# A gated feed-forward beside linear attention: the last 64 input rows of the first feed-forward product join its Strassen products

## The chip, the cores and the metric

The kernel runs on one core of a Trainium2 chip. A core has a matrix engine (TensorE, in the profile PE, its weight loads PEld), three engines for elementwise work (VectorE or DVE, ScalarE or ACT, GpSimd or POOL) and SyncE (SP), which here issues every data transfer (DMA). Each engine runs its own instructions in order and waits for the others on semaphores. Operands lie in an on-chip memory of 128 partitions; TensorE writes its results into banks of a second memory, PSUM, 512 fp32 values a partition each. The metric is the device time of one execution in microseconds.

## The reference

The input is x, 2048 tokens of 576 values. Cut to what matters:

```python
xn = layernorm(x)                       # [2048, 576]
q, k, v = split(xn @ wqkv)              # 32 heads of 18
s = linear_attention(phi(q), phi(k), v) @ wo
h = gelu(xn @ w1 + b1)                  # w1: [576, 4608], the first feed-forward product
g = silu(h @ w2 + b2)                   # w2: [4608, 576]
out = x + s * g
```

The change touches `xn @ w1` (its inner dimension is 576 = 512 + 64) and the place where `b2` is added.

## The kernel before

**Precision.** All matrix products are made from fp32 values split in two reduced-precision halves: `hi` is the value cast down (ScalarE), `lo` is what the cast lost (a VectorE difference of the value and `hi`). A product is hi x hi + hi x lo + lo x hi, three matmuls for every block of 128 inner rows.

**Stages.** First loop over 16 tiles of 128 tokens: layernorm, transposes, k, v, the state of the attention; meanwhile operands of w2 are prepared and stored. Second loop, `for i in range(1, NT + 4)`: queries, denominators, the attention output; beside it (function `beside(i, k)`, tables `SUMS` and `SPLITS`) the sums of token blocks that the feed-forward part needs. Then the feed-forward part: 18 steps. The tokens are handled in two halves of 1024; half 0 of the loop (steps 0 to 8) works on tokens 1024 to 2047, whose operands are on chip, and the other 1024 tokens' operands lie in DRAM (`x_dram`) and are loaded at the end of step 8 (`load_x_part`). A step makes 512 of the 4608 columns of h: two "up" products (class `Up`, 256 columns of w1 each), then a "down" product with the matching rows of w2 (function `product`), summed in `macc`.

**Strassen products.** Up and down products use a Winograd form of Strassen's scheme: seven products of sums of blocks in place of eight products of blocks. In an up product the two blocks of columns are `f0`, `f1`, the two blocks of 512 tokens are 0 and 1, and the inner dimension is split in A (rows 0 to 255) and B (rows 256 to 511). The weight sums 5, 6, 7, 4 are differences made by GpSimd (method `T`: T5 = f1A - f0A, T6 = f1B - T5, T7 = f1B - f1A, T4 = f0B - T6); "a" holds f0 itself (products 1 and 2), "b" the B part of f1 (product 3). The seven products are issued in the order `UP = (1, 6, 7, 5, 2, 3, 4)`. Product 1 goes into bank A and is copied by ScalarE to `m1_sb`; product 2 is added in the same bank. Product 6 and m1 give u1, product 7 and u1 give u2 (VectorE). Product 5 goes into bank E; VectorE adds it and u2 into B; then product 3 is accumulated on bank E.

**The last 64 rows.** 576 = 512 + 64, and the 64 rest rows are outside the scheme: with hi and lo stacked in one tile of 128 partitions, each of the four results gets two more matmuls (`rest` in `mm`: products 5, 2, 3 and 4). The difference of the two token blocks that product 3's bank needs is made by `XSums.rest`.

**Weights.** In steps 0 to 8 each 256 columns of w1 are prepared once (class `W1`: raw load, `T`, `hi`, `lo`) and stored to DRAM; steps 9 to 17 load the ready operands (`W1Loaded`). The plan of a step has 28 slots: slots 0 to 6 and 7 to 13 follow the products of its two up products, slots 14 to 27 the fourteen pieces of the down product. `P1` says in which slots the second operand of this step is prepared (during the first up product), `P0` where the first operand of the next step is. What is planned in a slot is issued after the product of that slot and what reads it. `in_order` fixes the order of VectorE, ScalarE, GpSimd and TensorE as issued; the transfers on SP are ordered by a scheduler. The lines to follow in the profile: L817 up matmuls, L834 copy of m1, L843 addition into B, L616 hi casts, L619 lo differences, L641, L643, L646, L649 T5, T6, T7, T4, L948 down matmuls, L955 their addition to `macc`, L337 and L341 token sums and their splits.

**The down product** has its own seven products in the order `ORDER = (1, 2, 7, 4, 5, 3, 6)`; 2, 4 and 3 are accumulated on the banks of 1, 7 and 5 after VectorE has read those. Each is made in two pieces of 256 tokens, each one bank pair out of three. In the first chunk of a half `macc` is begun: by a copy, or with the bias b2 (`BIAS`, a broadcast tile `b2b`).

Of the kernel before, what the change touches and what calls it, by code (L numbers as in the profile page):

```python
# [24 lines left out]
KT = 5  # L25
NF = F // P
# [13 lines left out]
def linear_attention_gated_ffn(ctx, tc, x, wqkv, wo, w1, b1, w2, b2, out):  # L40
# [4 lines left out]
    w1r = ctx.enter_context(tc.tile_pool(name="w1r", bufs=2))  # L45
# [32 lines left out]
    def stage_w1(name):  # L78
        return w1r.tile([P, 2 * KT * P], F32, tag="stw", name=name)

# [13 lines left out]
    b2b = pers.tile([P, D], F32, name="b2b")  # L94
# [19 lines left out]
    x_dram = dram.tile([P, 31, 512], F32, name="x_dram")  # L114
# [13 lines left out]
    wkvp = ph1.enter_context(tc.tile_pool(name="wkvp", bufs=1, reuse_waits="tile"))  # L128
    w2p = ph1.enter_context(tc.tile_pool(name="w2p", bufs=2, reuse_waits="tile"))
# [30 lines left out]
    def load_x(t):  # L160
        xraw[t] = stage_w1(f"x{t}")[:, :D] if t < 2 else stage(D, f"x{t}")
        nc.sync.dma_start(xraw[t], x[t * P : (t + 1) * P, :])
# [127 lines left out]
    def w2_hi(j):  # L290
        shape = [P, 2, 2, HD]
        if j % 4 < 2:
            w2op[j] = w1r.tile(shape, F32R, tag="stw", name=f"w2o{j}")
        else:
            w2op[j] = w2p.tile(shape, F32R, tag="w2o", name=f"w2o{j}")
        nc.scalar.copy(w2op[j][:, 0], w2_block(j // 3, T_OPS[j % 3])[0])
# [17 lines left out]
    class XSums:  # L314
# [8 lines left out]
        def place(self, in_place):  # L323
            A, B = self.A, self.B
            if in_place:
# [3 lines left out]
                self.xd = self.h0[:, 4]  # L329
            else:  # L330
                s2, s1, s4 = self.tiles = x_hi(0, "s2"), x_lo(0, "s1"), x_lo(1, "s4")
                self.s1, self.s2, self.s4 = ((t[:, A], t[:, B]) for t in (s1, s2, s4))
                self.xd = s2[:, 4]
# [30 lines left out]

        def rest(self, k):
            if k == 0:
                self.v = v, w = stage(512, "xv"), stage(512, "xw")
                self.tt(v, self.h0[:, 4], self.h1[:, 4], SUB)
                nc.sync.dma_start(w[:64], v[64:])
                nc.sync.dma_start(w[64:], v[:64])  # L370
                return
            (v, w), xd = self.v, self.xd
            if k == 1:
                self.tt(v, v, w, ADD)
            else:
                nc.scalar.copy(xd, v)
                self.tt(xd[64:], v[64:], xd[64:], SUB)

    def tmp_w1(name):
        return as2(stage_w1(name)[:, :1024])  # L380
# [29 lines left out]
    for t in range(NT):  # L410
# [43 lines left out]
        if t in (4, 8):  # L454
            b = t // 4 - 1
            if b == 0:
                nc.sync.dma_start(x_dram[:, 0:5], xh[0].bitcast(F32))
                nc.sync.dma_start(x_dram[:, 5:9], xl[0].bitcast(F32))
            else:
                nc.sync.dma_start(x_dram[:, 11:14], xh[1][:, 2:].bitcast(F32))  # L460
                nc.sync.dma_start(x_dram[:, 16:18], xl[1][:, 2:].bitcast(F32))
    xsum[0] = XSums(0, tmp_w1)
    xsum[0].sum1(0)
    nc.sync.dma_start(b1c, b1)
    nc.sync.dma_start(b2b, bass.AP(tensor=b2.tensor, offset=b2.offset, ap=[[0, P], [1, D]]))
# [12 lines left out]

    w1p = ctx.enter_context(tc.tile_pool(name="w1p", bufs=2, reuse_waits="tile"))
    w2rp = ctx.enter_context(tc.tile_pool(name="w2rp", bufs=1, reuse_waits="tile"))  # L480

    def load_w2_raw(n):
        raw = w2rp.tile([P, CF // 2, 2, 2, HD], F32, tag="w2raw", name=f"w2raw{n}")
        nc.sync.dma_start(raw.rearrange("p a b n d -> p (a b n d)"), w2[n % NC])
        return raw

# [57 lines left out]
    def normalize(t):  # L544
# [16 lines left out]
        if t:  # L561
            beside(t, 1)
# [47 lines left out]
    def keep_op(table, key, t, shape):  # L610
        d = dram.tile([P, 2, *shape], F32, name="op_" + "_".join(str(k) for k in key))
# [8 lines left out]

    class W1:


        def __init__(self, n):
# [3 lines left out]
            r4 = raw.rearrange("p (n k c) -> p n k c", n=2, k=KT)  # L628
            self.f0, self.f1 = r4[:, 0], r4[:, 1]
            self.src = {"a": self.f0, "b": self.f1[:, 2:]}  # L630
            self.ops, self.tiles = {}, {}

        def T(self, i):

            a, b = slice(0, 2), slice(2, 4)
            f0, f1, src = self.f0, self.f1, self.src
            tt = EW1.tensor_tensor
            if i in (5, 6):
                src[i] = w1p.tile([P, 2, P], F32, tag=f"w1t{i}", name=f"w1t{i}", bufs=1)
            if i == 5:  # L640
                tt(src[5], f1[:, a], f0[:, a], op=SUB)  # L641
            elif i == 6:
# [652 lines left out]
```

## Time and profile before

| | us |
|---|---|
| three runs | 1112.8, 1112.86, 1113.61 (median 1112.86) |
| the profiled execution | 1112.83 |
| its span, first to last instruction | 1111.0 |
| 0 to about 150 | first loop |
| about 150 to 290 | second loop |
| about 290 to 674 + 22 | steps 0 to 8 |
| about 696 to 1080 | steps 9 to 17 |
| after 1080 | the last down product and the output |

The granted TensorE clock was 0.999 of full speed. A row of a timeline gives start, length, engine, line, operation, output and inputs with their shapes, and in brackets how long the engine had been idle and what ended that. A row of waits gives who waited for whom, the total, how often and the longest. Instructions of one engine that follow closely overlap in the records by some hundredths of a microsecond, and matmuls by more, since they are pipelined; so the distance between starts is the price of a matmul.

### The profile page before, as it was taken

To read this page: it belongs to the slowest core of one execution; us is meant where nothing else is said; L and a number is where in the kernel's file an instruction comes from. 1 tells how busy PE (TensorE), PEld (TensorE's weight loads), DVE (VectorE), ACT (ScalarE), POOL (GpSimd) and SP (SyncE) were. 2 spreads that over 40 slices of the span, in tenths; PEclk is the share of its full clock that TensorE was granted. 3 is DMA by queue.
4 is the path that set the end of the run, shared out by engine and by line. 5 is a ranking of instruction groups with operands and counts; after the bars stand their busy time and mean duration, and the time that the engine had idled before them with its cause. 6 is when DMAs were issued, how large, how long until landed. Compare 5 with 4: busy or idle time off the path is not lost.

```text
span 1111.0 us, 18615 instructions
## 1 busy us (share of the span) xinstructions
PE 1101.8 (99%) x7008; PEld 1024.7 (92%) x7008; DVE 811.3 (73%) x1184; ACT 456.4 (41%) x800; POOL 448.8 (40%) x366
## 2 busy tenths in 40 slices
PE   8999999999999999999999999999999999999998
PEld 8999999999898998989989899899898998989987
DVE  6666657888697887988879878666475574764866
ACT  4444444233554354454544545524233242242342
POOL 4556534233354552553535524324234143242340
PEclk9999999999999999999999999999999999999999
DMA  7588631152757649476485679977666666666252
GB/s 298 190 334 301 237 123 44 71 215 93 283 227 282 239 176 356 162 264 243 182 333 184 231 283 397 353 251 263 227 207 211 206 203 213 228 201 222 83 164 101
DMA packets 83223, 246.71 MB, mean 222 GB/s; under 512 B 9213, under 2 KB 19709, under 8 KB 79551
## 3 DMA queue, kind: packets, MB, share of 16 engines
q1 hardware_dynamic: 83135, 245.54, 61.8%
q8 instruction: 55, 0.90, 0.3%
q14 instruction: 33, 0.27, 0.1%
HBM read 151.62 MB, written 92.47 MB: 220 GB/s over the span
## 4 chain that ended last, share of the span: by engine, by line
PE 95%; DVE 3%; POOL 1%; ACT 0%; DMA 0%; issue 0%; SPq 0%; POOLq 0%; DVEq 0%; ACTq 0%
PE pm L948 34%; PE e L817 12%; PE a L817 10%; PE zy L817 10%; PE pv L219 5%; PE pk L219 5%; PE b L817 4%; PE pq L219 4%; PE ps_s L592 4%; PE pd L1068 2%; PE ps_kva L256 1%; PE pt L196 1%; PE ps_kw L518 1%; PE ptp L574 1%; DVE xt L337 0%; DMA w<-wqkv 0%
## 5 line engine op out<-in xcount | busy, mean ns | idle before, releaser
L955 DVE TENSOR_TENSOR macc<-pm,macc 128x576 f32<-128x576 f32 x218 | 164.3, 754 | 56.8 <-PE pm L948 56.2
L616 ACT CAST h_h<-g 128x512 fp32r<-128x512 f32 x204 | 120.8, 621 | 139.9 <-PE pm L948 138.8
L619 DVE TENSOR_TENSOR h_l<-g,h_h 128x512 fp32r<-128x512 f32 x204 | 161.4, 798 | 0.0
L916 POOL TENSOR_TENSOR mid<-g 128x512 f32<-128x512 f32 x34 | 44.1, 1296 | 164.2 <-ACT g L825 164.2
L825 ACT ACTIVATE g<-b,b1c 128x512 f32<-128x512 f32 x36 | 24.8, 688 | 112.8 <-DVE b L843 112.7
L910 POOL TENSOR_TENSOR g<-g 128x512 f32<-128x512 f32 x34 | 55.0, 1618 | 34.1 <-DVE h_l L619 32.8
L834 ACT COPY mid<-a 128x512 f32<-128x512 f32 x36 | 21.1, 586 | 109.3 <-PE a L817 109.3
L837 DVE TENSOR_TENSOR mid<-b,mid 128x512 f32<-128x512 f32 x36 | 24.8, 690 | 46.5 <-PE b L817 35.4
L817 PE MATMUL a<-h0r,wa 128*128 128x512 f32 x180 | 58.6, 390 | 0.0
L817 PE MATMUL a<-xh,wa 128*128 128x512 f32 x180 | 58.5, 390 | 0.0
L913 POOL TENSOR_TENSOR g<-g 128x512 f32<-128x512 f32 x34 | 55.3, 1626 | 2.7
L1043 POOL TENSOR_TENSOR fin1l<-fin1h,fin1l 128x288 f32<-128x288 f32 x8 | 6.5, 808 | 119.4 <-DMA fin1l<-s_dram 76.5
L641 POOL TENSOR_TENSOR w1t<-w1raw 128x256 f32<-128x256 f32 x18 | 17.6, 978 | 81.5 <-DVE w L619 81.5
L817 PE MATMUL zy<-h1r,w 128*128 128x512 f32 x144 | 50.2, 389 | 0.0
L817 PE MATMUL zy<-xh,w 128*128 128x512 f32 x144 | 50.2, 389 | 0.0
L907 POOL TENSOR_TENSOR g<-g 128x512 f32<-128x512 f32 x34 | 47.6, 1401 | 2.7
L619 DVE TENSOR_TENSOR h_l<-mid,h_h 128x512 fp32r<-128x512 f32 x34 | 44.4, 1307 | 1.2
L825 ACT ACTIVATE g<-e,b1c 128x512 f32<-128x512 f32 x36 | 24.8, 688 | 49.5 <-DVE e L850 49.5
L555 POOL TENSOR_TENSOR pbuf<-phiq,den 128x576 f32<-128x576 f32 x16 | 20.2, 1262 | 59.0 <-DVE den L554 52.7
L850 DVE TENSOR_TENSOR e<-e,mid 128x512 f32<-128x512 f32 x36 | 25.1, 697 | 24.0 <-PE e L817 23.4
L288 POOL TENSOR_TENSOR w2r<-w2r 128x576 f32<-128x576 f32 x27 | 41.7, 1551 | 0.7
L817 PEld LDWEIGHTS a<-h0r,wa 128*128 128x128 f32 x180 | 33.8, 188 | 6.8
(776 smaller groups left out, 3530.9 us busy)
## 6 DMA issues: line engine op xcount, KB each, us to landing
op<-w SPq DMA_DIRECT2D x72, 256.0 KB
w<-op SPq DMA_DIRECT2D x72, 256.0 KB
op<-w2o SPq DMA_DIRECT2D x27, 576.0 KB
w2raw<-w SPq DMA_DIRECT2D x10, 1152.0 KB
w1raw<-w SPq DMA_DIRECT2D x18, 640.0 KB
op_a<-wa SPq DMA_DIRECT2D x18, 640.0 KB
wa<-op_a SPq DMA_DIRECT2D x18, 640.0 KB
w2r<-w SPq DMA_DIRECT2D x9, 1152.0 KB
```

Of the source, the lines that this page charges most:

```text
L219: nc.tensor.matmul(ps[:, h, :HD], st, w[:, k, h * HD : (h + 1) * HD], start=(i == 0), stop=(i == len(seq) - 1),)
L592: nc.tensor.matmul(ps[:, h, :HD], st[:, k, :], w[:, k, h * HD : (h + 1) * HD], start=(i == 0), stop=(i == len(seq) - 1),)
L616: nc.scalar.copy(pair[0], src)
L619: eng.tensor_tensor(pair[1], src, pair[0].bitcast(F32), op=SUB)
L817: nc.tensor.matmul(ps, st, mv, start=first and n == 0, stop=n == len(seq) - 1, skip_group_check=True,)
L825: nc.scalar.activation(g, ps, AF.Gelu_apprx_tanh, bias=b1c[:, f : f + 1])
L907: tt(src[5, pr], A(1, 0), A(1, 1), op=ADD)
L910: tt(src[6, pr], src[5, pr], A(0, 0), op=SUB)
L913: tt(src[3, pr], A(0, 1), src[6, pr], op=SUB)
L916: tt(src[7, pr], A(0, 0), A(1, 0), op=SUB)
L948: nc.tensor.matmul(ps[:, q, :HD], hs[p][st][:, cs], m[:, p, :], start=(n == 0 and i not in CHAIN), stop=(n == len(seq) - 1), skip_group_ch ...
L955: nc.vector.tensor_tensor(dst, src, dst, op=ADD)
```

## The change

The 64 rest rows are cut in two halves of 32, one for block A and one for block B of the inner dimension, so that all seven products have them. One matmul of 128 rows carries a rest: weight rows are (hi, hi, lo, zeros), token rows are (hi, lo, hi, hi), 32 each. So every product has 3 + 3 + 1 matmuls.

- The host lays w1 out with six blocks of 128 rows in place of five (each rest three times, and zeros). `T` works on three blocks in place of two. T5 is written over f0's columns in the raw tile; its tile `w1t5` is gone. `lo` makes one difference on the two full blocks and one on partitions 64 to 95 of the rest block.
- `P1` moves T5 and T6 from slot 0 to 1 and the split of 6 from slot 1 to 2.
- The token rests: class `Rest` collects them through DRAM, makes the sums for products 5, 3 and 6 with a column of signs, splits them and stores hi and lo (`rq_dram`). `load_rest` loads one product's 128 rows: hi in all four quarters, then lo over the second quarter. `RESTS` says at which token tile each piece is done; `XSums.rest` is gone.
- `macc` holds b2 from the start: `start_with_b2` writes it by DMA at slot 1 of step 0 and slot 7 of step 9.
- Pools move to make room, the first token sum moves from the end of the first loop to i = 4 of the second, and the scratch for dynamic DMA is halved.

```diff
-            a, b = slice(0, 2), slice(2, 4)
+            a, b = slice(0, 3), slice(3, 6)
             f0, f1, src = self.f0, self.f1, self.src
             tt = EW1.tensor_tensor
-            if i in (5, 6):
-                src[i] = w1p.tile([P, 2, P], F32, tag=f"w1t{i}", name=f"w1t{i}", bufs=1)
             if i == 5:
+                src[5] = f0[:, a]
                 tt(src[5], f1[:, a], f0[:, a], op=SUB)
             elif i == 6:
+                src[6] = w1p.tile([P, 3, P], F32, tag="w1t6", name="w1t6", bufs=1)
                 tt(src[6], f1[:, b], src[5], op=SUB)
...
         def lo(self, i):
-            set_lo(self.ops[i], self.src[i], EL1)
-            keep_op(w1_dram, (self.n, i), self.tiles[i], [W1_K[i], P])
+            t, src = self.tiles[i], self.src[i]
+            if i == "a":
+                two = lambda v: v.rearrange("p (h k) c -> p h k c", h=2)
+                hi, src, lo = two(t[:, :6]), two(src), two(t[:, 6:])
+            else:
+                hi, src, lo = t[:, None, :3], src[:, None], t[:, None, 3:]
+            EL1.tensor_tensor(lo, src[:, :, :2], hi[:, :, :2].bitcast(F32), op=SUB)
+            r = hi[64:96, :, 2]
+            EL1.tensor_tensor(r, src[64:96, :, 2], r.bitcast(F32), op=SUB)
+            keep_op(w1_dram, (self.n, i), t)
...
+        def split(self, k):
+            src = (self.q, self.e)[k]
+            h, l = (self.tmp("wt", f"{k}{v}")[:, :512] for v in "hl")
+            nc.scalar.copy(h, src)
+            nc.vector.tensor_tensor(l, src, h.bitcast(F32), op=SUB)
+            nc.sync.dma_start(rq_dram[self.half, k, 0], h.bitcast(F32))
+            nc.sync.dma_start(rq_dram[self.half, k, 1], l.bitcast(F32))
+
+        def sums(self):
+            e, g, m, up = self.e, self.g, self.m, slice(64, P)
+            nc.vector.scalar_tensor_tensor(e, self.f, sgn[:, 0:1], e, op0=MUL, op1=ADD)
+            nc.vector.scalar_tensor_tensor(e[up], g[up], sgn[up, 1:2], e[up], op0=MUL, op1=ADD)
+            nc.vector.tensor_tensor(e[64:96], e[64:96], m[64:96], op=SUB)
...
+    def load_rest(half, i, dst):
...
+        nc.sync.dma_start(
+            dst, bass.AP(tensor=hi.tensor, offset=hi.offset, ap=[[0, 4], [512, 32], [1, 512]])
+        )
+        nc.sync.dma_start(dst[32:64], lo)
...
+    RESTS = {
+        3: (0, ("gather",)), 4: (0, ("whole",)), 6: (0, ("split",)), 8: (0, ("sums", "split")),
+        9: (1, ("gather",)), 11: (1, ("whole",)), 13: (1, ("split",)), 15: (1, ("sums", "split")),
+    }
...
+    def start_with_b2():
+        for b in range(2):
+            nc.sync.dma_start(
+                macc[:, :, 2 * b : 2 * b + 2].rearrange("p q h d -> p q (h d)"),
+                bass.AP(tensor=b2.tensor, offset=b2.offset, ap=[[0, P], [0, QH], [1, D]]),
+            )
...
-            if rest:
-                seq += [(v, self.xr[rest[1]]) for v in self.w.rest(rest[0])]
+            seq.append((wr, r))
...
     P1 = dict(
-        T={5: 0, 6: 0, 7: 1, 4: 2},
-        hi={"a": 0, 6: 1, 7: 2, 5: 3, "b": 4, 4: 4},
-        lo={"a": 0, 6: 1, 7: 2, 5: 3, "b": 4, 4: 4},
+        T={5: 1, 6: 1, 7: 1, 4: 2},
+        hi={"a": 0, 6: 2, 7: 2, 5: 3, "b": 4, 4: 4},
+        lo={"a": 0, 6: 2, 7: 2, 5: 3, "b": 4, 4: 4},
     )
```

255 lines of the change are left out of this document (145 added, 110 removed), and 2 rows, old and new, of the table SUMS.

## The prediction

> **What bounds the kernel now.** I read the busy shares first, then the chain that ended last, then what TensorE waited for.
>
> ```profile
> PE 1101.8 (99%) x7008; PEld 1024.7 (92%) x7008; DVE 811.3 (73%) x1184; ACT 456.4 (41%) x800; POOL 448.8 (40%) x366
> ...
> PE 95%; DVE 3%; POOL 1%; ACT 0%; DMA 0%; issue 0%; SPq 0%; POOLq 0%; DVEq 0%; ACTq 0%
> ```
>
> TensorE is busy 99% of the span and makes 95% of the chain. VectorE has 27% idle over the whole span, which hides that its stages differ. The waits of TensorE show how little it ever stands still; beside the first microseconds of the kernel this is the longest row:
>
> ```profile
> PE pq L219 <- DVE phiq L229: 0.4, 1, 0.4
> ```
>
> So time leaves this kernel where matmuls leave it, and it is added where something makes TensorE wait. The chain in order of time gives the period of a feed-forward step (start, length, what):
>
> ```profile
> 493.69 22.43 PE pm L948 x168
> 538.83 22.43 PE pm L948 x168
> ...
> 719.33 22.39 PE pm L948 x168
> 764.43 22.39 PE pm L948 x168
> ```
>
> Two neighbouring down products of the first half start 45.14 us apart, two of the second half 45.10. A step is 168 down matmuls (22.4 us) and two up products of 50 matmuls, 22.7 us. The timeline of TensorE in one up product (start, length) prices a matmul:
>
> ```profile
> 561.09 0.40 PE L817 MATMUL a<-xh,wa 128*128 128x512 f32 x1
> ...
> 568.85 1.98 PE L817 MATMUL e<-s,wb 128*128 128x512 f32 x8
> 570.66 0.39 PE L817 MATMUL zy<-xh,w 128*128 128x512 f32 x1
> ...
> 573.83 1.52 PE L817 MATMUL b<-s,w 128*128 128x512 f32 x6
> 575.19 0.39 PE L817 MATMUL zy<-xh,w 128*128 128x512 f32 x1
> ```
>
> Product 3 (8 matmuls) starts at 568.85 and the next product at 570.66; product 6 (6 matmuls) takes 573.83 to 575.19. Both give 0.2265 us a matmul. The step starts at 561.09, product 3 comes 7.76 us later.
>
> **What goes.** Each up product has 7 x 7 = 49 matmuls in place of 7 x 6 + 4 x 2 = 50, with the same 512 moving columns. 36 of them: 36 x 0.2265 = 8.2 us off the path. No bound is needed here: TensorE is the chain. The bias adds of the first chunk were VectorE additions and stay so, with another second operand: 0. ScalarE casts 2688 columns a weight where it cast 2048 and is busy 41%; DMA makes 0% of the chain, and stores and loads 192 KB more a weight; six small memsets on GpSimd (40%) and a smaller DMA scratch lie beside the path: 0 each, except where the next parts find them on it.
>
> **What the first half pays: a chain that stood beside the path is put into it.** In the first half every step prepares its second W1 operand while its first up product runs (table P1). Before, the GpSimd differences T5, T6, T7 waited for no split of that weight. Now T5 writes over columns that the split of "a" (ScalarE copy, VectorE difference) still reads, so T5 comes after it, T6 reads T5, and T7 stands behind T6 on GpSimd. I follow one step, started at 561.09 - 45.14 = 515.95. ScalarE (copy of M1, then casts; 128x384 at the end), VectorE, GpSimd:
>
> ```profile
> 517.54 0.59 ACT L834 COPY mid<-a 128x512 f32<-128x512 f32 x1 [5.66 <-PE a L817]
> 518.03 0.73 ACT L616 CAST wa<-w1raw 128x640 fp32r<-128x640 f32 x1
> 518.65 0.41 ACT L616 CAST w<-w1t 128x256 fp32r<-128x256 f32 x1
> ...
> 525.03 0.51 ACT L616 CAST wb<-w1raw 128x384 fp32r<-128x384 f32 x1
> ```
>
> ```profile
> 518.79 0.82 DVE L619 TENSOR_TENSOR wa<-w1raw,wa 128x640 fp32r<-128x640 f32 x1 [0.53 <-ACT wa L616]
> ...
> 520.13 0.64 DVE L619 TENSOR_TENSOR w<-w1t,w 128x256 fp32r<-128x256 f32 x1
> ...
> 521.30 1.05 DVE L619 TENSOR_TENSOR w<-w1raw,w 128x256 fp32r<-128x256 f32 x1
> 522.27 0.69 DVE L843 TENSOR_TENSOR b<-e,mid 128x512 f32<-128x512 f32 x1
> ...
> 526.05 0.42 DVE L619 TENSOR_TENSOR w<-w1raw,w 128x256 fp32r<-128x256 f32 x1
> ...
> 539.47 0.68 DVE L619 TENSOR_TENSOR h_l<-g,h_h 128x512 fp32r<-128x512 f32 x1
> ```
>
> ```profile
> 516.05 0.74 POOL L641 TENSOR_TENSOR w1t<-w1raw 128x256 f32<-128x256 f32 x1 [10.04 <-DVE w L619]
> ...
> 517.94 0.92 POOL L646 TENSOR_TENSOR w1raw<-w1raw 128x256 f32<-128x256 f32 x1
> 519.76 0.74 POOL L649 TENSOR_TENSOR w1raw<-w1raw,w1t 128x256 f32<-128x256 f32 x1 [0.90 <-DVE wa L619]
> ...
> 532.68 1.29 POOL L907 TENSOR_TENSOR g<-g 128x512 f32<-128x512 f32 x1
> ```
>
> Before: copy of M1 517.54, cast of "a" 518.03, its difference 518.79 to 519.61, T4 0.15 later at 519.76. T5 to T7 had run from 516.05 to 518.86. So the differences of 6 and 7 were ready, and the addition into B (522.27) ended at 522.97. Product 3 writes on the bank that this addition reads, and was due at 515.95 + 7.76 = 523.71: 0.74 us to spare.
>
> After: product 1 has seven matmuls, so the copy of M1 starts 0.23 later, 517.77, the cast of "a" at 518.26. It has 768 columns in place of 640; (0.73 - 0.41) / 384 us a column makes 0.84, end 519.10. The difference is now one of 512 columns (0.68, the h_l row) and one of 2x128 on 32 partitions (0.42, the last row of a w; the rows of one engine overlap by 0.07): end 520.16. GpSimd starts 0.15 later, 520.31, with 384 columns each, between 0.74 (256) and 1.29 (512): 1.02. T5, T6, T7 end at 523.37. Cast of 7: 0.51, end 523.88. Its difference 0.42 and the new short one, for which the nearest row is a 64x128 in another stage:
>
> ```profile
> 264.73 0.29 DVE L580 TENSOR_TENSOR th<-ptp,th 64x128 fp32r<-64x128 f32 x1
> ```
>
> 0.29, so 524.52 with the overlap. In VectorE's order the addition into B stands behind both differences, as before: 0.69, end 525.2. Product 3 is now due at 515.95 + 5 x 7 x 0.2265 = 523.88. TensorE waits 1.3 us, with nothing colliding. VectorE and GpSimd do collide: the 256 column difference takes 0.42 alone and 0.64 or 1.05 beside GpSimd above, and T4 now runs beside the last two differences. One such collision adds 0.2 to 0.6, two of the larger size make the upper bound 2.6. I take 1.7, one collision of the middle size, since one of the two differences of 7 certainly meets T4. Nine steps: 15.3 us, bounds 11.7 and 23.
>
> What is queued behind the waiting addition: the gelu of B on ScalarE, then the casts of 5, "b", 4 and W2, and their differences. These have the second up product to arrive in; I price them in the next part.
>
> [...]
>
> **Arrears of VectorE in the down products, first half.** Per W1, six short differences are new (0.42 + 5 x 0.29 = 1.9 us) and 2048 columns of difference become 1792 (0.3 off): 3.2 us a step on an engine that the page shows at 73% and that is nearly full here:
>
> ```profile
> 533.42 0.70 DVE L843 TENSOR_TENSOR b<-e,mid 128x512 f32<-128x512 f32 x1 [0.20 <-PE e L817]
> ...
> 540.45 0.76 DVE L955 TENSOR_TENSOR macc<-pm,macc 128x576 f32<-128x576 f32 x1 [0.30 <-PE pm L948]
> 541.13 1.22 DVE L619 TENSOR_TENSOR wa<-w1raw,wa 128x640 fp32r<-128x640 f32 x1
> 542.26 0.75 DVE L955 TENSOR_TENSOR macc<-pm,macc 128x576 f32<-128x576 f32 x1
> ```
>
> The first down product's bank is read at 540.45, right when it is full. TensorE accumulates into that bank again one product (1.60) later, so VectorE may be 1.60 - 0.75 = 0.85 late at most. At 542.26 it is 0.23 late. Now the up product that leads here ends 0.25 us sooner and its product 5 ends 0.45 later, so 6.8 us of VectorE work from 533.42 to 540.15 has 0.7 less room, of which 0.3 was idle; the short difference of "a" adds 0.42, and the late start of the step and longer GpSimd work the rest. That is 1.2 to 1.4 late against 0.85 allowed, and the next gaps hold 0.68 + 1.05 of work in 1.60, so a second bank is late too. I take 0.9 a step for the eight steps that prepare an "a" there, 7.2 us. Bounds: 0 (the idle found elsewhere suffices) and 1.6 in eight steps, 13.
>
> **The last tokens of the attention stage.** The rests' sums are put on VectorE ahead of the token-15 denominators. These rows are from VectorE, GpSimd, VectorE and TensorE's weight load:
>
> ```profile
> 274.68 1.21 DVE L337 TENSOR_TENSOR xu<-xu,xl 128x1024 f32<-128x1024 f32 x1
> ...
> 277.33 1.17 POOL L555 TENSOR_TENSOR pbuf<-phiq,den 128x576 f32<-128x576 f32 x1 [3.65 <-DVE den L554]
> ...
> 278.22 0.83 DVE L337 TENSOR_TENSOR xv<-xh,xh 128x512 f32<-128x512 f32 x1
> ...
> 278.55 0.53 PEld L574 LDWEIGHTS ptp<-ident,pbuf 128*128 128x128 f32 x5 [0.30 <-POOL pbuf L555]
> ```
>
> Today GpSimd's pbuf, which needs those denominators, already keeps TensorE waiting 0.30. New before it: three 128x512-wide operations and a difference, nearest row xv at 0.83 and h_l at 0.68, and between them a ScalarE copy:
>
> ```profile
> 284.94 0.62 ACT L376 CAST s<-xv 128x512 fp32r<-128x512 f32 x1
> ```
>
> 4 x 0.66 + 0.62 = 3.3 us, and a split of 0.68 two tokens earlier that finds no idle time to vanish in. What is removed there (xv, xw) stood behind the denominators. I take 3.5; bounds 0 (sums scheduled into gaps) and 5. The same group for the other half, tokens 3 to 8, and the sum moved out of the first stage meet VectorE gaps of about a microsecond a token and no waiting bank: 0, at most 1, inside that bound.
>
> **The middle.** Transfers fill the DMA engines around the half change (columns: stretch, busy times, clock, DMA share, GB/s):
>
> ```profile
> 650.00:700.00 50.00, 50.00 (x296) 45.42 (x295) 40.84 (x57) 23.15 (x39) 20.62 (x15) 1.00 0.97 375
> 700.00:716.00 16.00, 16.00 (x73) 13.23 (x71) 7.77 (x13) 8.99 (x13) 3.22 (x3) 1.00 1.05 393
> 716.00:718.00 2.00, 2.00 (x10) 1.69 (x9) 1.97 (x2) 1.07 (x2) 1.92 (x2) 1.00 0.68 257
> 718.00:720.00 2.00, 2.00 (x13) 1.77 (x13) 1.86 (x4) 1.31 (x2) 0.68 (x1) 1.00 0.09 34
> ```
>
> New there: seven rest loads of 320 KB against three of 256 (1.5 MB), 192 KB more for each of three weights, and the bias by DMA, 2.4 MB: 4.5 MB at 393 GB/s, 11 us. The engines ran empty at about 717.5 (the last two rows), so the bias lands near 725 to 729. Its first reader follows the third down product, 719.33 + 4.8 = 724.1, and may be some 2.4 late (the bank it frees is wanted two products on, 3.2, less its own 0.75). I take 2.5; bounds 0 and 8. SP also waits at each rest load's second half for its first; other transfers are then in flight, so I price that inside these bounds. The bias load at the start of the feed-forward part has over 15 us: 0.
>
> **Sum**, against the profiled execution's own 1112.83 us (span 1111.0 plus 1.8 around it; the median shown is 1112.86): 1112.8 - 8.2 + 15.3 + 7.2 + 3.5 + 2.5 = 1133. The second half keeps its 0.45 a step, since no weight is prepared there.
>
> **Rivals.** (a) The matmuls go and nothing waits: 1112.8 - 8.2 = 1104.6. For it: TensorE is the chain and other engines look idle. Against: it needs the addition into B to end by 523.88, and the chain above ends 1.3 us too late without a collision. Chance 0.09. (b) Only the W1 chain costs, the rest is absorbed: 1112.8 - 8.2 + 11.7 or 15.3 = 1116 or 1120. It decides from 0.9 us a step on, where 9 steps outweigh 8.2. For it: VectorE finds idle time elsewhere. Chance 0.2. (c) Collisions throughout, or the middle waits for the bias: 23 + 13 instead of 15.3 + 7.2 gives 1147, with a late middle (8 for 2.5) 1152. For it: the 1.05 row. Against: the 0.42 and 0.64 rows, which collide little. Chance 0.13. [...]
>
> (d) Near balance, 1111 to 1115, if the step loses about 0.9: chance 0.03. My forecast, the sum with its parts moved some microseconds: 0.55.
>
> The range 1113 to 1150 takes in (b) and most of (c) and leaves (a) out. Faster by over 0.2% (2.2 us, about what a measurement of this kernel tells from nothing) 0.09, within it 0.03, slower 0.88.
>
> **What would show it.** In the changed profile: 36 fewer up matmuls and second-half steps of about 44.65 us; first-half steps of 46 to 48; TensorE waits at the up line put down to VectorE's addition into B, nine of 1.3 to 2.6 us; GpSimd waits of T5 for VectorE's "a"; TensorE waits at pm for macc of some tenths; at token 15 a wait of 3 to 4 us on pbuf. I am wrong if first-half steps take under 45.1 us, which means that T5 or B is not held as I read it; or if the time is lost in the attention stage or the middle rather than in the first half.

## The result and the profile after

Four runs of the changed kernel took 1213.32 to 1214.74 us, median 1214.46, beside 1112.92 for the kernel before (four runs): a ratio of 1.0909, 95% interval 1.089 to 1.0928. The profiled execution's span is 1211.5 us against 1111.0, its mean granted TensorE clock 0.973 against 0.999. The forecast was 1133, its range ended at 1150: the sign was right, the size five times too small.

The page of the changed kernel, busy shares and the chain by engine:

```profile
PE 1129.1 (93%) x6972; PEld 1035.2 (85%) x6972; DVE 863.7 (71%) x1298; ACT 469.9 (39%) x802; POOL 462.5 (38%) x372
...
PE 70%; DVE 10%; DMA 9%; issue 4%; ACT 3%; POOL 2%; SPq 1%; DVEq 0%; ACTq 0%; POOLq 0%
```

The 36 matmuls are gone (7008 to 6972), yet TensorE has fallen from 95% of the chain to 70%, with VectorE and DMA in its place. Where that happens is seen when the span is cut at the first matmul of each step, as TensorE's timeline gives it. Windows of the changed kernel, steps 0, 4, 9 and 12 (stretch, length, busy times with instructions of TensorE, its weight load, VectorE, ScalarE and GpSimd, granted clock, DMA share, GB/s):

```profile
298.36:352.70 54.34, 48.15 (x269) 41.80 (x267) 39.50 (x59) 24.32 (x42) 22.82 (x17) 0.97 0.90 321
507.02:558.43 51.41, 47.08 (x268) 41.94 (x267) 43.33 (x67) 22.42 (x40) 22.89 (x17) 0.97 0.62 224
762.13:842.83 80.70, 52.58 (x269) 45.98 (x268) 31.20 (x42) 19.25 (x28) 14.70 (x10) 0.83 0.75 270
932.83:977.82 44.99, 44.99 (x269) 40.80 (x267) 28.26 (x38) 14.58 (x24) 15.24 (x13) 1.00 0.68 219
```

The same windows of the kernel before, steps 5 and 9:

```profile
515.95:561.09 45.14, 45.14 (x271) 41.18 (x269) 38.08 (x55) 21.13 (x40) 21.34 (x17) 1.00 0.65 240
696.46:741.55 45.09, 45.09 (x270) 41.14 (x269) 31.67 (x42) 19.09 (x28) 15.01 (x10) 1.00 0.84 310
```

With all steps cut in this way the 100.5 us are accounted for:

| piece | before | changed | difference |
|---|---|---|---|
| start of step 0 | 290.27 | 298.36 | +8.1 |
| step 0 | 45.09 | 54.34 | +9.3 |
| steps 1 to 7, each | 45.14 | 51.36 | 7 x 6.22 = +43.5 |
| step 8 | 45.10 | 49.89 | +4.8 |
| step 9 | 45.09 | 80.70 | +35.6 |
| steps 10 to 16, each | 45.10 | 45.00 | 7 x -0.10 = -0.7 |
| step 17 to the end | 53.74 | 53.68 | -0.1 |

What TensorE waited for in the changed kernel (total, times, longest):

```profile
PE e L901 <- DVE b L927: 26.3, 9, 3.3
PE pm L1031 <- DVE macc L1040: 13.2, 8, 5.7
PE e L901 <- DMA rx<-rq_dram: 12.2, 1, 12.2
PE zy L901 <- DMA l1r<-x_dram: 4.9, 1, 4.9
PE pm L1031 <- issue: 4.7, 1, 4.7
PE ptp L560 <- POOL pbuf L543: 3.8, 1, 3.8
PE zy L901 <- DMA xh<-rq_dram: 2.5, 1, 2.5
PE ps_s L578 <- ACT s L583: 1.6, 1, 1.6
```

The forecast's places are there: eight waits for the addition into B, some for macc, one for pbuf. Rows 3 to 5 and the 5.7 of row 2 are step 9, where nearly nothing was forecast; row 7 is step 0, where a product waits for its rest load. The 5.7 are the bias: in the same view VectorE waits for its transfer.

```profile
DVE macc L1040 <- DMA macc<-b: 5.3, 1, 5.3
```

VectorE between lo("a") and the addition into B, in the step that starts at 558.43 (start, length):

```profile
561.61 0.69 DVE L657 TENSOR_TENSOR wa<-w1raw,wa 128x512 fp32r<-128x512 f32 x1 [0.23 <-ACT wa L648]
...
565.56 0.68 DVE L657 TENSOR_TENSOR w<-w1t,w 128x256 fp32r<-128x256 f32 x1 [1.31 <-ACT w L648]
566.25 0.99 DVE L659 TENSOR_TENSOR w<-w1t,w 32x128 fp32r<-32x128 f32 x1
567.28 1.51 DVE L657 TENSOR_TENSOR w<-w1raw,w 128x256 fp32r<-128x256 f32 x1
568.80 0.28 DVE L659 TENSOR_TENSOR w<-w1raw,w 32x128 fp32r<-32x128 f32 x1
569.12 0.70 DVE L927 TENSOR_TENSOR b<-e,mid 128x512 f32<-128x512 f32 x1
```

GpSimd beside it, the sum T4 and then a sum of w2 (L954):

```profile
565.91 1.19 POOL L644 TENSOR_TENSOR w1raw<-w1raw,w1t 128x384 f32<-128x384 f32 x1
567.06 1.45 POOL L954 TENSOR_TENSOR w2raw<-w2raw 128x576 f32<-128x576 f32 x1
```

TensorE at the end of it, and the windows of one microsecond there:

```profile
569.87 2.93 PE L901 MATMUL e<-s,wb 128*128 128x512 f32 x6 [3.26 <-DVE b L927]
```

```profile
568.00:569.00 1.00, 0.00 (x0) 0.00 (x0) 0.99 (x2) 0.00 (x0) 0.51 (x1) 1.00 1.03 433
...
571.00:572.00 1.00, 1.00 (x4) 0.81 (x3) 0.94 (x3) 1.00 (x3) 0.00 (x0) 0.50 0.03 10
572.00:573.00 1.00, 1.00 (x3) 0.73 (x3) 0.96 (x3) 1.00 (x4) 0.00 (x0) 0.50 0.38 154
573.00:574.00 1.00, 1.00 (x6) 0.79 (x5) 0.95 (x3) 0.48 (x1) 0.00 (x0) 0.98 1.06 418
```

The short difference of 32x128 takes 0.28 us alone (568.80) and 0.99 beside GpSimd's sums, the 128x256 one 0.41 to 0.43 alone and 1.51. The three that are stretched end 0.14 to 0.28 us after the GpSimd sum beside them: 566.24 after T7's end at 565.96, 567.24 after T4's at 567.10, 568.79 after the w2 sum's at 568.51. So the addition into B ends late, TensorE stands for 3.26 us, and its clock is 0.50 for 3.41 us, from 569.62 on: three or four matmuls a microsecond in place of six.

The windows by step give 4.33 of the 51.41 us as idle (3.26 here, 1.08 at macc) and 47.08 as busy, 2.09 more than the 44.99 that the same matmuls need in step 12. Not all of the 2.09 is lost to the clock. In step 1 of e5_whole, a kernel described below in which steps 1 to 7 are the same program, a wait of the same length left the clock at 1.00:

```profile
363.25 1.63 PE L896 MATMUL e<-s,wb 128*128 128x512 f32 x6 [3.25 <-DVE b L922]
```

```profile
351.82:402.81 50.99, 45.88 (x268) 40.68 (x267) 43.33 (x67) 22.40 (x40) 22.88 (x17) 1.00 0.64 229
```

This step takes 50.99 us, and step 1 of the changed kernel, with the halved clock, 51.44. So the halved clock makes TensorE 1.2 us busier, but the step's other waits are then 1.1 instead of 1.9 us, which fits a VectorE that catches up meanwhile. The step loses 0.45 us by the clock, and nearly 6 us over step 12 without it.

In step 9, SyncE's queue issues the rest loads (start, length, line, operation):

```profile
756.74 0.54 SPq L752 DMA_DIRECT2D h1r<-rq_dram  x1
...
768.79 0.32 SPq L755 DMA_DIRECT2D h1r<-rq_dram  x1
...
770.09 5.68 SPq L752 DMA_DIRECT2D rx<-rq_dram  x4
779.50 8.60 SPq L755 DMA_DIRECT2D rx<-rq_dram  x4
```

and two windows there:

```profile
776.00:782.00 6.00, 0.00 (x0) 0.00 (x0) 0.00 (x0) 0.00 (x0) 0.00 (x0) 0.94 0.31 104
782.00:788.00 6.00, 0.00 (x0) 0.00 (x0) 0.00 (x0) 0.00 (x0) 0.00 (x0) 0.50 0.29 102
```

L752 is a rest's first transfer (hi, four times), L755 the second (lo), which waits until the first has landed: 768.79 is 12 us after 756.74, SyncE's wait there is 10.2 us, and all that SyncE would issue next waits with it. For twelve microseconds nothing runs on the core but rest loads, at 102 to 104 GB/s and 0.3 of the DMA engines.

### The profile page after: what moved, and what is told of

It is laid out like the page before. It is cut to its first block, busy times and chain, and to the rows that moved or that the text cites. A ratio compares the mean times of both kernels' runs of the same rounds, so it can differ in the third digit from the quotient of the medians.

```text
span 1211.5 us, 18780 instructions
## 1 busy us (share of the span) xinstructions
PE 1129.1 (93%) x6972; PEld 1035.2 (85%) x6972; DVE 863.7 (71%) x1298; ACT 469.9 (39%) x802; POOL 462.5 (38%) x372
## 4 chain that ended last, share of the span: by engine, by line
PE 70%; DVE 10%; DMA 9%; issue 4%; ACT 3%; POOL 2%; SPq 1%; DVEq 0%; ACTq 0%; POOLq 0%
PE pm L1031 26%; PE e L901 8%; PE zy L901 7%; PE a L901 6%; PE pv L221 5%; PE pk L221 5%; PE b L901 3%; PE pq L221 3%; DMA op<-w 2%; PE ps_s L578 2%; PE pd L1143 2%; DVE h_l L605 2%; DMA rx<-rq_dram 1%; DVE w L657 1%; PE ps_kva L258 1%
## 5 line engine op out<-in xcount | busy, mean ns | idle before, releaser
L1040 DVE TENSOR_TENSOR macc<-pm,macc 128x576 f32<-128x576 f32 x234 | 176.2, 753 | 68.7 <-PE pm L1031 53.5
L635 POOL TENSOR_TENSOR w1raw<-w1raw 128x384 f32<-128x384 f32 x18 | 21.9, 1215 | 132.1 <-issue 115.4
L994 POOL TENSOR_TENSOR g<-g 128x512 f32<-128x512 f32 x34 | 52.7, 1551 | 39.7 <-DVE h_l L605 38.4
L901 PE MATMUL e<-s,wb 128*128 128x512 f32 x108 | 38.0, 500 | 26.5 <-DVE b L927 26.3
L901 PE MATMUL zy<-xh,w 128*128 128x512 f32 x162 | 55.9, 398 | 2.5 <-DMA xh<-rq_dram 2.5
L901 PE MATMUL zy<-h1r,w 128*128 128x512 f32 x162 | 55.3, 396 | 0.7 <-DVE macc L1044 0.7
L997 POOL TENSOR_TENSOR g<-g 128x512 f32<-128x512 f32 x34 | 55.0, 1617 | 2.7
L901 PEld LDWEIGHTS e<-s,wb 128*128 128x128 f32 x108 | 24.7, 238 | 36.1 <-DVE b L927 30.8
L901 PE MATMUL a<-h0r,wa 128*128 128x512 f32 x162 | 55.6, 397 | 0.0
L901 PE MATMUL a<-xh,wa 128*128 128x512 f32 x162 | 55.4, 396 | 0.0
L991 POOL TENSOR_TENSOR g<-g 128x512 f32<-128x512 f32 x34 | 46.6, 1372 | 2.7
L927 DVE TENSOR_TENSOR b<-e,mid 128x512 f32<-128x512 f32 x36 | 25.2, 699 | 30.8 <-PE e L901 30.2
```

The source lines that it names most:

```text
L901: nc.tensor.matmul(ps, st, mv, start=first and n == 0, stop=n == len(seq) - 1, skip_group_check=True,)
L927: tt(B, E, u2_sb, op=ADD)
L991: tt(src[5, pr], A(1, 0), A(1, 1), op=ADD)
L994: tt(src[6, pr], src[5, pr], A(0, 0), op=SUB)
L997: tt(src[3, pr], A(0, 1), src[6, pr], op=SUB)
L1040: nc.vector.tensor_tensor(dst, src, dst, op=ADD)
```

## The experiments

Times are those of single runs beside 1214.5 for the changed kernel, unless an interval is given. All that follow start from the changed kernel. Some runs also lose time in the first 20 us of the kernel, which their edits do not touch: e7_w2pool 3.2 us, e3_own5 2.8, e13_best2 1.2 and e11_t2 1.1, all within the column "step 0 starts". The steps tell more than the times. They are cut as above:

| kernel | step 0 starts | step 0 | steps 1 to 7 | step 9 | time |
|---|---|---|---|---|---|
| changed | 298.4 | 54.3 | 51.4 | 80.7 | 1214.5 |
| e2_late67 | 297.5 | 56.3 | 49.5 | 83.1 | 1201.6 |
| e3_own5 | 300.2 | 56.6 | 50.8 | 79.8 | 1212.1 |
| e6_no_r | 297.5 | 57.9 | 46.7 | 82.2 | 1180.8 |
| e7_w2pool | 301.3 | 56.7 | 49.7 | 80.6 | 1206.6 |
| e10_rpool | 297.5 | 58.9 | 48.1 | 83.7 | 1194.5 |
| e11_t2 | 299.6 | 57.5 | 46.1 | 83.1 | 1179.8 |
| e1_parted | 298.3 | 50.9 | 51.3 | 83.2 | 1212.4 |
| e5_whole | 298.7 | 53.2 | 51.5 | 57.5 | 1190.5 |
| e15_quarters | 298.4 | 51.4 | 51.3 | 69.7 | 1199.2 |
| e4_nobias | 297.8 | 54.2 | 51.4 | 66.5 | 1198.6 |
| e8_b2tile | 297.7 | 54.5 | 51.3 | 69.0 | 1201.0 |
| e14_early | 296.0 | 59.3 | 51.6 | 80.3 | 1216.8 |
| e9_comb | 297.2 | 49.5 | 49.5 | 45.0 | 1156.9 |
| e12_best | 298.3 | 55.5 | 48.1 | 45.0 | 1153.6 |
| e13_best2 | 298.4 | 48.1 | 48.1 | 45.0 | 1145.2 |

### The first half's steps

```diff
 P1: T={5: 1, 6: 1, 7: 1, 4: 2},
-    hi and lo: {"a": 0, 6: 2, 7: 2, 5: 3, "b": 4, 4: 4}
+    hi and lo: {"a": 0, 6: 3, 7: 3, 5: 4, "b": 4, 4: 5}
```

> Only the order of VectorE and ScalarE in the first half is changed: hi and lo of operands 6 and 7 of the next W1 come one slot later (slot 3, behind the addition into B), 5 and 4 one slot later too; T5 stays in place. Theory (the addition into B stands in VectorE's order behind lo6 and lo7, which wait for GpSimd; the stall of 3.3 us then halves TensorE's clock for some 3 us): no TensorE wait for b in steps 1 to 8, clock 1.00 there, step 51.4 -> 45.2 to 46.7 us, time 1214.5 - 8 x (4.7 to 6.2) = 1165 to 1177 us. Rival (VectorE is simply late, the wait only moves to macc or to the lo of h in the down products): steps 49 to 51 us, time 1198 to 1212 us.

The wait for B and the halved clock are gone, but the step only falls to 49.5: the rival's number. One step of e2_late67, by windows and by waits:

```profile
502.21:551.70 49.49, 45.92 (x268) 40.70 (x267) 42.51 (x67) 22.20 (x40) 22.69 (x17) 1.00 0.64 235
```

```profile
PE a L901 <- ACT mid L918: 1.6, 1, 1.6
PE pm L1031 <- DVE macc L1040: 1.1, 1, 1.1
PE pm L1031 <- DVE h_l L605: 0.4, 1, 0.4
PE e L901 <- DVE b L927: 0.4, 1, 0.4
```

VectorE still has 42.5 us of work in a step (38.1 before), and the wait comes back in four places. So the order alone isn't the cause.

```diff
 T, i == 5:
-    src[5] = f0[:, a]
+    src[5] = t5p.tile([P, 3, P], F32, ...)   (n >= 1)
 P1: T={5: 0, 6: 0, 7: 1, 4: 2}; hi and lo: 6 at 1, 7 at 2 (as before the change)
```

> T5 gets its own tile again for every W1 but the first, and the slots are those of the kernel before (T5 and T6 in slot 0, 6 split in slot 1, 7 in slot 2). Theory (the in-place T5, which has to wait for lo of a, starts the chain that makes the stall): steps 1 to 8 at 45 to 47 us, no wait for b over 1 us, time 1165 to 1180 us. Rival (the collisions of VectorE and GpSimd make the stall whatever the start of the chain, since both add three k-rows instead of two): a wait of 2 us or more stays, steps 49 to 51 us, time 1198 to 1212 us.

The theory falls. T5 no longer waits for lo("a"), yet the wait for B stays at 2.7 us and the step at 50.8. VectorE now collides with GpSimd's T6 and T7 further ahead: the two differences of "b", 0.41 and 0.29 us in the changed kernel, take 0.73 and 1.01. The chain that ended last stays on VectorE from 559.45 to the end of the addition at 570.54. TensorE in e3_own5:

```profile
570.60 2.31 PE L904 MATMUL e<-s,wb 128*128 128x512 f32 x6 [2.69 <-DVE b L930]
```

The in-place T5, on which the forecast built its chain, is worth half a microsecond a step. Behind this wait of 2.69 us the clock was 0.50 too, from 571.36 on, when the matmuls had begun again; behind the same wait in steps 1 and 8 it stayed at 1.00.

```diff
 e2_late67, and in lo:
-    EL1.tensor_tensor(r, src[64:96, :, 2], r, op=SUB)
```

> The order of e2_late67, and the subtractions that make lo of the 32 rest rows (12 instructions of VectorE in a step of the first half) are left out, so that the stacked rows hold hi in place of lo. Theory (VectorE is late: 42.5 us of work in a step of 45, against 38.1 before; these instructions are 12 x 0.28 us and more): steps 1 to 8 fall from 49.45 us to 45.2 to 47, time 1201.6 - 8 x (2.5 to 4.2) = 1168 to 1182 us. Rival (the chain GpSimd, ScalarE, VectorE with its collisions sets the step, not VectorE's load): steps above 48.5 us, time 1194 to 1202 us.

The theory holds. The kernel leaves out the lo of the rest rows, so it shows what this work costs and not a version to use. The step of e6_no_r is

```profile
495.48:542.18 46.70, 45.71 (x268) 40.77 (x267) 37.89 (x55) 22.21 (x40) 23.10 (x17) 1.00 0.68 248
```

Twelve short instructions gone, VectorE's work 4.6 us shorter and back at the 38 of before, the step 2.8 us shorter. That VectorE's load makes the larger part of what e2_late67 left is shown.

```diff
 e6_no_r, and in T (also for 7 and 4):
-    tt(src[5], f1[:, a], f0[:, a], op=SUB)
+    tt(src[5][:, :2], f1[:, :2], f0[:, :2], op=SUB)
```

> e6_no_r, and GpSimd's sums 5, 7 and 4 of W1 run over two k-rows instead of three (the stacked rows of these operands are left unsummed). Theory (the third row makes GpSimd's sums half as long again, and what VectorE does beside them is stretched): steps 1 to 8 fall from 46.7 us to 45.1 to 46.0, time 1168 to 1175 us. Rival (what is left of the 1.6 us over the step before is the order of ScalarE and VectorE, not GpSimd's length): steps at 46.4 us or more, time 1178 to 1182 us.

Steps of 46.1 us, between the two: 0.6 for GpSimd's third row. The time, 1179.8, lies in the rival's range. This kernel leaves work out as well. The last 1.1 us over the 45.0 of the second half were not taken apart.

Moving work from VectorE to GpSimd:

```diff
 e2_late67, and in W2.lo (e7_w2pool):
-    set_lo(..., nc.vector)
+    set_lo(..., nc.gpsimd)
 e2_late67, and in W1.lo (e10_rpool):
-    EL1.tensor_tensor(r, ...)
+    EW1.tensor_tensor(r, ...)
```

> The order of e2_late67, and lo of W2's operands (four of 0.76 us in a step of the first half) moves from VectorE to GpSimd. Theory (VectorE's load): steps 1 to 8 fall from 49.45 us to 46 to 48, time 1176 to 1192 us. Rival (what GpSimd takes over collides with VectorE and stands in front of T and S): steps at 49 us or longer, time 1199 to 1212 us.

> The order of e2_late67, and lo of the 32 rest rows (12 small instructions in a step of the first half) is made by GpSimd instead of VectorE. Theory (VectorE's load alone, as e6_no_r showed 2.7 us a step for it): steps 1 to 8 at 46.7 to 47.5 us, time 1180 to 1188 us. Rival (as in e7_w2pool, GpSimd gives back what VectorE gains, since the instructions wait for ScalarE in GpSimd's order and hold up the sums behind them): steps at 48.5 us or longer, time 1194 to 1206 us.

e7_w2pool gains nothing: four instructions fewer on VectorE (63 for 67 a step), and its busy time rises from 42.51 to 42.84, so what stays there takes longer, while GpSimd's work grows from 22.7 to 28.7 us a step.

e10_rpool lies between the theories in its steps, 1.4 us of the 2.8 that leaving the work out gave, and with 1194.5 at the lower edge of the rival's time.

### The rest loads

```diff
 load_rest (e1_parted):
-    dst <- hi rows, leading dimension [0, 4]
-    dst[32:64] <- lo
+    dst[0:32] <- hi;  dst[32:64] <- lo
+    dst[64:] <- hi rows, leading dimension [0, 2]
```

> Rest loads parted so that no transfer writes rows that another one writes: rows 0-31 hi, rows 32-63 lo, rows 64-127 hi twice, three transfers instead of two, and so no wait of SyncE for the landing of the first. Theory (SyncE's wait for its own transfer, and all that is queued behind it, makes the losses at the first and at the tenth feed-forward step: +8.1 us before the first Up, +9.3 in step 0, +35.6 in step 9): step 9 falls from 80.7 us to 50-62, step 0 from 54.3 to 46-50; steps 1 to 7 stay at 51.4; time 1178 to 1195 us. Rival (the bytes are the bound there, not the waits: DMA share 0.8 with seven x parts, seven rests and two sets of W1): step 9 stays above 72 us, time 1203 to 1214 us.

SyncE's wait for its own transfer is gone, and step 9 is 2.5 us longer: the theory falls for the middle, and holds only for step 0 (-3.4). While such rests run alone, e1_parted has

```profile
772.00:778.00 6.00, 5.50 (x12) 3.65 (x12) 0.69 (x1) 0.00 (x0) 0.00 (x0) 0.53 0.18 59
```

59 GB/s, slower than with four. So the transfers themselves are slow.

```diff
 split (e5_whole): stores hi, lo, hi, hi to rq_dram[half, k, :, 32 v : 32 v + 32]
 load_rest: dst <- rq_dram[half, k, at], 128 rows in one transfer
```

> Rests stored in DRAM as the products need them (hi, lo, hi, hi for each product: four stores for a split instead of two) and loaded by one transfer of 128 rows instead of a repeating one of 128 rows and one of 32. New theory (in the stretch 776 to 788 us nothing but rest loads ran, at 98 GB/s and 0.26 of the DMA engines, and parting them gave nothing: transfers that read 32 rows over and over, or write only 32 partitions, are slow, and seven rests cost 13 us and more of queue in step 9): no TensorE wait for rx over 3 us, step 9 falls from 80.7 us to 62 to 72, step 0 by 2 to 6, time 1190 to 1205 us. Rival (what lacks is a free place in the queue, the rests come after the x parts and W1 whatever their form): step 9 above 77 us, time 1207 to 1217 us (the four stores more could cost).

In step 9 better than expected: no wait for rx there, up products of 22.8 us (43.9 in the changed kernel), step 9 at 57.5, -23.2. In step 0 worse: TensorE still waits 4.4 us for a rest, and the step falls by 1.2 us instead of 2 to 6. While the rests of step 9 are loaded, the DMA engines are full now:

```profile
750.00:755.00 5.00, 5.00 (x40) 5.00 (x39) 4.76 (x8) 2.24 (x4) 0.00 (x0) 1.00 1.04 401
```

```diff
 load_rest (e15_quarters):
+    for v, part in enumerate((hi, lo, hi, hi)):
+        dst[32 v : 32 v + 32] <- part
```

> Each rest load is four plain transfers of 32 rows (hi, lo, hi, hi into the four quarters of the partitions), none with a repeating leading dimension, none overlapping another. [...] Rival (32 rows into 32 partitions are slow however they are written): step 9 above 74 us, time 1205 to 1216 us.

With the repeating dimension as the cause, step 9 was expected at 56 to 64 us and the time at 1188 to 1200. Between that and the rival again: step 9 at 69.7, the time of 1199.2 within the first range. Its up products fall from 43.9 to 29.3 us and the wait for rx from 12.2 to 2.9, so the repeating dimension is the larger part. But the sixteen transfers of the last four rests keep SyncE for 13.8 us, 6.9 of them in three waits between transfers, and the bias comes later still (9.3 us at macc in place of 5.7).

The transfer records show how many packets were under way at a time: in the changed kernel, with a leading dimension of four, exactly four for 7.9 of the 12 us from 776 to 788; in e1_parted, with one of two, exactly two for 4.4 of the 6 us from 772; in e5_whole, with plain loads, 16 to 21 all through 750 to 755. The shares of the 16 DMA engines in these stretches are 0.30, 0.18 and 1.04. In these three the packets under way go with the repeating dimension; what ties them to it was not shown.

### The bias

```diff
 product (e4_nobias; e8_b2tile in brackets):
-    if c == 0 and i == 1: copy
+    if c == 0 and i in (1, 2, 7, 4, 3): copy   [i == 1: copy; 2, 7, 4, 3: product + b2b]
-    add(1, start_with_b2);  add(base + 7, start_with_b2)   [b2b, a tile of 128 x 576, loaded once]
```

> The bias is left out (no transfer of b2 into the accumulators; the first product into each of C11, C22, C21 and C12 is copied instead of added). Theory (in step 9 the two b2 transfers stand in SyncE's queue behind the stores of the first half's accumulators, and the first additions wait for them: 5.7 us at macc and the two pieces of 4.8 and 4.3 us behind it, with the clock at 0.50): step 9 falls by 8 to 14 us, step 0 by 0 to 3, time 1199 to 1207 us. Rival (the wait is for the copy of the accumulators to DRAM and the bias only the last in line, so that the same pieces stay): time 1211 to 1215 us.

> b2 lies in a tile of its own in SBUF, loaded once ahead of step 0; the first product into C11, C22, C21 and C12 of either half is written as product plus b2 in one VectorE instruction, which replaces the addition into the accumulator. Nothing is left out. Theory (the b2 transfers into the accumulators alone make the 14.2 us that step 9 lost in e4_nobias): step 9 at 66 to 68 us, time 1197 to 1202 us. Rival (VectorE needs longer for a broadcast operand and the same waits come back at macc): time 1204 to 1212 us.

Step 9 gets 14.2 us shorter without the bias and 11.7 with it in a tile, so that its step 9 is 1 us longer than the theory's range; the 5.7 us at macc and the 4.7 behind them vanish. The addition from the tile costs VectorE what the other one did (0.75 us on average). Why the transfers are late is in the chain of e1_parted (start, length):

```profile
793.62 11.79 DMA c_dram<-macc
805.42 12.87 DMA macc<-b
```

The bias starts when the store of the accumulators has landed, and then takes 12.9 us. Without the bias step 0 starts 0.6 us earlier and is 0.2 shorter, with the tile it starts 0.7 earlier and is 0.1 longer: the forecast's 0 for the first bias load was right within a microsecond.

### The attention stage's end, and the sum of it

```diff
 RESTS (e14_early, e9_comb, e13_best2):
-    13: (1, ("split",)), 15: (1, ("sums", "split")),
+    12: (1, ("split",)), 13: (1, ("sums", "split")),
```

> The changed kernel with the second half's rest sums two tokens earlier in the attention stage (split at token 12, sums and second split at token 13 instead of 13 and 15), nothing else. Theory (VectorE's six added instructions at token 15 make the 3.8 us wait for pbuf, TensorE's clock halves behind it, and the rest loads of step 0 come late): no pbuf wait over 1 us, first Up at 294 to 297 us instead of 298.4, step 0 at 50 to 53 us instead of 54.3, time 1207 to 1212 us. Rival (step 0 is held up by SyncE's waits for its own rest loads whenever the sums are ready): first Up earlier by 1 to 3 us, step 0 within 1 us of 54.3, time 1211 to 1214 us.

Neither holds: 1216.8 lies above both. The pbuf wait is gone and another of 3.0 us (ps_s for ScalarE's s) is in its place. Step 0 starts 2.4 us earlier and is 5 longer. SyncE's queue in e14_early:

```profile
280.56 0.52 SPq L752 DMA_DIRECT2D xh<-rq_dram  x1
...
292.40 0.30 SPq L755 DMA_DIRECT2D xh<-rq_dram  x1
...
298.62 0.53 SPq L752 DMA_DIRECT2D xh<-rq_dram  x1
304.12 0.30 SPq L755 DMA_DIRECT2D xh<-rq_dram  x1
```

The rests are ready, and SyncE still stands between their halves until 304, ahead of step 0's stores and loads. Most of what step 0 loses it loses here: 3.9 and 1.1 us of waits for rests, and the halved clock behind them (0.91 in the mean of the step).

> The order of e2_late67, the rests of e5_whole and the b2 tile of e8_b2tile together, and the second half's rest sums of the attention stage two tokens earlier (split at token 12, sums at 13). Nothing is left out. Theory (four separate losses): 1214.5 - 12.8 (order) - 24.0 (rests) - 13.4 (bias) - 3.8 (wait for pbuf) = 1160 us, within 1155 to 1166; step 9 at 45 to 47 us, steps 1 to 8 at 49.4. Rival (the losses of step 9 lie behind one another, so that the second is still met when the first is gone): step 9 above 52 us, time 1167 to 1180 us.

The theory holds: e9_comb is e2_late67, e5_whole, e8_b2tile and e14_early together and has step 9 at 45.0, step 0 at 49.5.

> The order of e2_late67, the rests of e5_whole, the b2 tile of e8_b2tile and lo of the rest rows on GpSimd as in e10_rpool. Nothing is left out. Theory (the losses of first half, rests and bias are separate): e9_comb's 1156.9 us less 8 to 9 steps x 1.35 = 1144 to 1147 us, within 1140 to 1150, about 3% slower than the kernel before; steps 1 to 8 at 48.1 us, step 9 at 45 to 46. Rival (the gain of e10_rpool came from a step that the other edits change): time above 1153 us.

Missed by 6.6 us and more; the time is that of the rival, for another reason than the rival's. The comparison with e9_comb left out that e12_best has the sums at token 15 again, and TensorE waits 7.1 us for a rest load in step 0. (Ratio to before 1.0362, interval 1.0345 to 1.0379.)

> e12_best with the second half's rest sums two tokens earlier. Nothing is left out. Theory (e12_best's step 0 of 55.5 us is the late rest load alone): no TensorE wait for rx, step 0 at 48 to 49.5 us, steps 1 to 8 at 48.1, time 1153.6 - 6 to 7.5 = 1145 to 1148 us. Rival (the subtractions on GpSimd delay the first stores, so that step 0 stays long): step 0 above 52 us, time 1150 to 1154 us.

1145.2 us, ratio 1.0283, interval 1.0266 to 1.03. The earlier sums, worth nothing alone, are worth 7 us of step 0 once the rests are loaded whole. Step 4 of e13_best2:

```profile
490.76:538.84 48.08, 45.90 (x269) 40.67 (x268) 39.45 (x55) 22.23 (x40) 31.61 (x29) 1.00 0.66 238
```

69 of the 101 us are undone. What is left is 3.0 us in each of steps 0 to 7, 2.2 in step 8, and the 8 us before step 0. What holds up these steps was not taken apart. No version was faster than the kernel before; with the second half's gain at 0.1 us a step there is little to win.

## Why the prediction was wrong

Of the 80 us that the forecast missed, 39.1 lie in steps 0 to 8, 33.6 in step 9, 4.6 ahead of step 0 and 2.8 in the steps after 9. Two prices of the sum failed most: that of the middle, where transfers were priced by their bytes, and that of the first half, where VectorE's work was priced as two separate waits.

- **36 matmuls, -8.2.** They went, but were worth 0.10 us a step instead of 0.45, where nothing waits. In step 12 the 98 up matmuls take 22.45 us, where 22.72 less two of 0.2265 makes 22.27, and the 168 unchanged down matmuls 22.54 instead of 22.38, at a clock of 1.00. Starts in TensorE's timeline show where: in the down product two distances, behind its fifth and sixth matmul, are 0.19 and 0.235 in place of 0.133; in the up products distances of 0.230 to 0.236 begin behind the rest matmul of product 5 and recur in products 2, 3 and 4, the last to be issued. So the term failed in the half where it was thought safest; the cause was not found. Every kernel with the change shows 45.0 there.
- **The wait for B, 1.7 a step.** The chain was timed well up to the cast of 7; then the forecast allowed one collision of VectorE with GpSimd, and there are three (0.68, 0.99 and 1.51 where the times alone add up to 1.13): 2.05 us on top of the 1.3 forecast without any makes 3.35; 3.26 were measured. The upper bound of 2.6 counted the 256-column differences only and not the short one, and it looked at T4 alone. The longest collision, 1.51, is with the w2 sum behind T4, and so was the 1.05 row of before, which the forecast used without naming its partner:

```profile
520.45 1.62 POOL L870 TENSOR_TENSOR w2raw<-w2raw 128x576 f32<-128x576 f32 x1
```

The rival (c) came nearest. And the forecast's origin of the wait was not needed for it: with T5 in a tile of its own 2.7 us stay (e3_own5).
- **What a wait costs.** The sum took a wait for its own length. The halved clock adds 0.45 us to a step of the first half, by the pairs of steps with and without it (51.44 and 50.99 in the changed kernel and e5_whole, 50.9 and 50.46 in e3_own5), and 2.5 us behind the wait for pbuf, where it lasts 6.8 us instead of 3.4. Of the 2.09 us that TensorE is busier, 0.9 stay at full clock and were not taken apart. No row of before could show this, since there TensorE never stood still for long (0.4 us at the most after the kernel's first microseconds).
- **Arrears of VectorE, 0.9 a step.** 1.08 measured. Right in place and size, though VectorE's work grew by 5.2 us a step (38.08 to 43.33) where 3.2 were forecast; but e2_late67 and e6_no_r show that it is one face of a load which, with the wait for B removed, comes back elsewhere.
- **Attention stage, 3.5.** The wait for pbuf is 3.8, near the forecast. But step 0 starts 8.1 us later: matmul by matmul against before, TensorE loses 1.8 us at an earlier token, 3.8 at pbuf, and 2.5 behind it at a clock of 0.50. The 1.8 are the same group of sums for the other half, priced at 0: ScalarE's s, for which TensorE waits 1.6, stands behind the cast that waits for VectorE's sums.

```profile
223.20 0.62 ACT L733 CAST rest01h<-rest0ef 128x512 fp32r<-128x512 f32 x1 [6.08 <-DVE rest0ef L742]
223.73 0.63 ACT L583 COPY s<-ps_s 128x576 f32<-128x576 f32 x1
```

- **Step 0's transfers, 0, and the middle, 2.5.** The step that failed is "4.5 MB at 393 GB/s, 11 us", and with it "other transfers are then in flight, so I price that inside these bounds". The sign of the term was right, its size was not: the rests ran at 102 to 104 GB/s, SyncE's wait held back x parts and W1, the bias stood behind the accumulators' stores. The middle cost 35.6 us against a bound of 8; whole rest loads take back 23.2 of them (e5_whole), the bias in a tile 11.7 (e8_b2tile), and e9_comb, which has both, all of them (step 9 at 45.0). Step 0 cost 9.3; no term stood for its rest loads, and with the rests whole, ready earlier and the bias in a tile it is as long as the steps behind it (48.1 in e13_best2). Here the mechanism was seen and dismissed: the waits of the queue for itself were noted but not followed to what stood behind them.
- Of the signs listed, the macc waits were 1.1, not tenths; the pbuf wait was right; steps of 51.4 instead of 46 to 48 and a second half of 45.0 instead of 44.65 were not. "Or if the time is lost in the attention stage or the middle": 44 of the 101 us are, and 9 more in step 0.

## What to carry to other kernels

Where TensorE did not wait, two matmuls saved were worth 0.10 us a step against 0.45 of their own time. Each wait added cost its length and, behind most of 2.5 us and more, a clock of 0.50 for a while (half a microsecond in a step of the first half, 2.5 us at the end of the attention stage). So a small gain on TensorE must be weighed against every instruction that it puts on the next fullest engine. A transfer is to be priced by its shape and by its place in the queue, not by its bytes over the best rate: the same rests ran at 102 to 104 GB/s as repeating loads with nothing else under way, and as plain ones in a traffic of 401. Look at the outermost dimension of its patterns, at what it must wait for, and at everything that is issued behind it. VectorE, with 84% of a step's time in use (38 of 45 us), had little idle time to give, since its instructions stand in an order that others wait for: with 5.2 us more of its work in a step TensorE stood idle for 4.33.

## What was not expected of the hardware

- The length of a wait of TensorE did not settle whether its clock fell. The granted clock went to 0.50 for 3.4 us after waits of 2.48 us (changed kernel, step 0), 2.69 and 3.26, in several cases only when the matmuls had begun again; it stayed at 1.00 after waits of 2.70 (e3_own5, step 1), 2.97 (e14_early, at 264.6) and 3.25 us (e5_whole, step 1), as after waits of 1.6 and 1.1 us (e2_late67).
- A VectorE difference of 32x128 takes 0.28 us alone and 0.99 beside GpSimd: what is stretched ends 0.14 to 0.28 us after GpSimd's instruction, however short it is itself.
- A repeating load of 128 rows moved 102 to 104 GB/s, with four packets under way at a time; the same rows stored out in full and loaded plainly went with the rest of the traffic at 401 in all (e5_whole, 750 to 755).
